# Seven block products for eight in gate and value: five sixths of a two-layer feed-forward kernel rewritten by Strassen's identity

## The chip, the cores and the metric

One core of one Trainium2 chip runs the program. The metric is device time in microseconds (us) of one execution; three runs of the kernel before stand beside one profiled execution.

## The reference, cut to what matters

```python
attn = softmax(mean_of_pairs(q) @ k.T / 8) @ v            # 2 x 8 heads, 1152 keys, 576 pooled queries
x = elu(x @ w_in) @ w_out                                 # 1152 tokens, 512 -> 2048 -> 512
xn = x / sqrt(mean(x * x) + 1e-6) * rms_g
g, val = xn @ w_gate, xn @ w_val                          # 512 -> 1536 each
out = (g * sigmoid(g) * val) @ w_out2                     # 1536 -> 512
```

The change is in the last two lines: `g` and `val`, and how their product is handed to the last matrix product.

## The kernel before, in words

Activations lie transposed: features on the 128 partitions, tokens along the free axis, in three chunks `c` of 384 tokens (`cs(c)`). Every fp32 product is made of three matmuls on rounded parts: an operand is split into a high part `h` (a cast) and a low part `l` (the rest), and `product` (L161) adds wh·xh, wh·xl and wl·xh over four blocks of 128 features: 12 matmuls of 128x384 for one 128-wide output block and one chunk. `xh`, `xl` hold the split input, `x2` the unsplit one.

The weights come as 64-bit words. `Stream` (L73) loads 68 blocks of 128x512 in the order of use and turns each into its two parts, in small steps that the loops call between products (`ws.step`): two ACT operations (L113 into `wt`, L115 into `we`), three DVE operations (L119, L121, L124, the last giving the block in fp32), a cast on ACT (L140, `wh`) and a subtraction on POOL (`lo_pool`, L63, `wl`). Eight blocks can be ready at once. Each engine runs its own queue in the order in which the program issues; a queue stands behind an instruction that waits.

After the first layer the last loop (L633) finishes `x2` chunk by chunk, and `Norm` scales it: `sums` (L572: three small matmuls, Sqrt on ACT, reciprocal on DVE), `spread` (L581: three transposes that lay the factor over the partitions) and `scale` (L587: four multiplications on DVE, four casts on ACT, four subtractions). For the last chunk this lies inside the next stage: `unit(0, 0)` and `unit(0, 1)` run first, with `sums` in the middle of the second, then `spread`, then the rest.

Gate and value: 12 output blocks `i`, three chunks. `unit(i, c)` (L661) is a gate and a value product, 24 matmuls; `swiglu` (L648) makes Silu on ACT, the product with the value on DVE, and the two parts `uh`, `ul` of the result (L657 on ACT, a subtraction on POOL or DVE). The last product reads `uh`, `ul` (L687). Eight PSUM banks go round (`bank`, L542).

Of the kernel before, what the change touches and what calls it, by code (L numbers as in the profile page):

```python
# [1 line left out]

# [6 lines left out]
F32 = mybir.dt.float32  # L9
# [29 lines left out]
def tile_kernel(ctx: ExitStack, tc: tile.TileContext, qd, kd, vd, w1d, w2d, wgd, wvd, wod, rgd, outd):  # L39
# [33 lines left out]
    class Stream:  # L73


        def __init__(self, srcs):
            self.srcs = srcs
            self.loaded = self.done = self.at = 0
            self.alloc = False
            self.raw, self.parts = {}, {}  # L80
            self.pools = [(wp, NE)]
            self.ops = self.work()
# [14 lines left out]
        def work(self):  # L97
            tail = None
            for i in range(len(self.srcs)):
                if tail and not wide:  # L100
                    yield from tail
                self.load(i + 2)
                w = self.raw.pop(i)
                if wide:

                    lo, hi = w[:, :, 0], w[:, :, 1]  # L110
                    e = wp.tile([128, 512], U32, tag="we", name="we", bufs=2)
                    t = wp.tile([128, 512], U32, tag="wt", name="wt", bufs=2)
# [11 lines left out]
                    V.scalar_tensor_tensor(out=t, in0=hi, scalar=0x80000000, in1=t,  # L124
                                           op0=ALU.bitwise_and, op1=ALU.bitwise_xor)
                    self.load(i + 3)
                    yield
                    w = f(t)
                tail = self.split(i, w)
                yield  # L130
            yield from tail

# [234 lines left out]
    def emit_x(p, xs, a=0, b=QS):  # L367
# [7 lines left out]
        else:  # L375
# [9 lines left out]
                + [w[i] for i in range(12) for w in (wgd, wvd)] + [wod[i] for i in range(12)])  # L385
# [156 lines left out]
    def bank():  # L542

        nonlocal nbank
        n, nbank = nbank % 8, nbank + 1
        if n == 5 and len(psb) == 1:
            with tc.using_default_side("right"):
                psb.append(ctx.enter_context(tc.tile_pool(name="psC", bufs=3, space=PSUM)))
        return psb[n >= 5].tile([128, 512], F32, tag="b", name="b", bufs=3 if n >= 5 else 5)[:, 0:CH]

    gh, gl = (gp.tile([128, 8, NT], F32R, name=f"g{n}", tag=f"g{n}") for n in "hl")

    def g_quad(hf, q, c):
        return lambda k: ((ge[0][:, k], ge[1][:, k]) if hf == c == q == 0 and k < NE else
                          (gh[:, 4 * q + k, cs(c)], gl[:, 4 * q + k, cs(c)]))

    class Norm:
# [14 lines left out]
        def sums(self):  # L572
            b = bank()
# [7 lines left out]
        def spread(self):  # L581

            b = self.b = bank()
# [16 lines left out]
    for hf in range(2):  # L600
        for i in range(8):
            w = ws.get(wi)
            for c in range(3):
# [4 lines left out]
                elu(ps, gh[:, i, cs(c)], gl[:, i, cs(c)], lo_dve if c == 1 and hf else lo_pool)  # L608
# [39 lines left out]
    def swiglu(i, c, pg, pv, k=4):  # L648
        s = hp.tile([128, CH], F32, tag="e", name="sl", bufs=4)
        T.activation(out=s, in_=pg, func=AF.Silu)  # L650
        flush()
        ws.step(wi + 2 * i if i > 1 else wi, k)
        V.tensor_tensor(out=s, in0=pv, in1=s, op=ALU.mult)

        def parts():
            h, l = uh[:, i, cs(c)], ul[:, i, cs(c)]
            T.copy(h, s)  # L657
            (lo_dve if c == 1 else lo_pool)(l, s, h)
        pending.append(parts)
# [8 lines left out]

    mctx.close()
    first = [unit(0, 0), unit(0, 1, norms[2].sums)]  # L670
# [10 lines left out]
    units = [(1, 0), (1, 1), (0, 2), (1, 2)] + [(i, c) for i in range(2, 12) for c in range(3)]  # L681
    for i, c in units:
        swiglu(*unit(i, c))
        ws.step(wi if i < 2 else wi + 2 * i, 3)
    wi += 24
    flush()
    for m in range(4):  # L687
        bs = [bank() for c in range(3)]
        for k in range(3):
            w = ws.get(wi)  # L690
            for c in range(3):
                product(bs[c], w, lambda b: (uh[:, 4 * k + b, cs(c)], ul[:, 4 * k + b, cs(c)]), k == 0, k == 2)
                ws.step(wi, 4)
                if k == 2:
                    o = hp.tile([128, CH], F32, tag="e", name="o", bufs=4)
                    T.copy(o, bs[c])
                    SP.dma_start(out=outd[128 * m:128 * m + 128, cs(c)], in_=o)
            wi += 1
# [56 lines left out]
```

## Time and profile before

| | us |
|---|---|
| three runs: median (lowest, highest) | 686.81 (686.01, 686.85) |
| the profiled execution, its own time | 686.79 |
| its span in the profile | 685.0 |
| busy PE, share of the span | 675.8, 99% |
| busy DVE, ACT, POOL | 469.0, 447.7, 376.1 |

A busy share says how much of the span an engine had something in work; for PE, whose matmuls overlap, the distance between two starts is the price of one. Gate and value start at 454.74 us of the span and the last product at 605.80 us.

### The profile page before, as it was taken

Reading aid. Unit: us, or ns where it says so; the run is one execution under the profiler, and the core shown is the slowest. Engines: PE = TensorE matmul, PEld = TensorE weight load, DVE = VectorE, ACT = ScalarE, POOL = GpSimd, SP = SyncE. Lnnn points to the kernel's source line nnn. Section 1 sums busy time; section 2 is a strip of 40 time slices with the busy share of each in tenths; the row PEclk is TensorE's granted clock in tenths of the full one; section 3 lists DMA queues with packets and bytes.
Section 4 is the critical chain, followed back from the end, with each engine's and each line's share of the span. In section 5 each row is a group of like instructions: output and inputs, shape, how many; then the busy total and the mean of one; then the engine's idle time right before and its main releaser. Section 6 shows DMA issues by size and latency. Waiting matters only on the chain.

```text
span 685.0 us, 11443 instructions
## 1 busy us (share of the span) xinstructions
PE 675.8 (99%) x4243; PEld 666.9 (97%) x4243; DVE 469.0 (68%) x752; ACT 447.7 (65%) x923; POOL 376.1 (55%) x335
## 2 busy tenths in 40 slices
PE   7999999999999999999999999999999999999997
PEld 6999999999999999999999999999999999999997
DVE  5989998998999875788557676377865655563000
ACT  5978889898988968885557875356655554453000
POOL 5798888898988415784324454464544443342000
PEclk9999999999999999999999999999999999999999
DMA  5522333233233001223421213112232222231000
GB/s 182 206 90 88 105 133 123 89 103 118 88 106 117 1 1 63 77 78 123 151 96 61 94 63 123 48 45 92 94 124 93 94 95 91 91 119 70 35 35 34
DMA packets 21608, 62.34 MB, mean 91 GB/s; under 512 B 2736, under 2 KB 4784, under 8 KB 21552
## 3 DMA queue, kind: packets, MB, share of 16 engines
q1 hardware_dynamic: 21552, 61.62, 26.8%
q8 instruction: 33, 0.54, 0.3%
q14 instruction: 23, 0.19, 0.1%
HBM read 59.25 MB, written 2.36 MB: 90 GB/s over the span
## 4 chain that ended last, share of the span: by engine, by line
PE 93%; POOL 3%; DMA 1%; ACT 1%; issue 1%; SPq 1%; POOLq 0%; ACTq 0%
PE b L166 20%; PE b L167 20%; PE b L168 20%; PE s L278 10%; PE o L322 10%; PE t L296 9%; DMA rawk<-in_k_dram 1%; POOL kd L63 1%; POOL vd L63 1%; PE t L357 1%; ACT p L287 1%; POOL qt L63 0%; POOL rawq L242 0%; PE fb L166 0%; PE fb L167 0%
## 5 line engine op out<-in xcount | busy, mean ns | idle before, releaser
L166 PE MATMUL b<-xh,wh 128*128 128x384 f32 x468 | 157.2, 336 | 0.0
L168 PE MATMUL b<-xh,wl 128*128 128x384 f32 x468 | 157.1, 336 | 0.0
L167 PE MATMUL b<-xl,wh 128*128 128x384 f32 x468 | 157.0, 335 | 0.0
L63 POOL TENSOR_TENSOR wl<-wt,wh 128x512 fp32r<-128x512 f32 x68 | 94.8, 1394 | 75.4 <-ACT wh L140 42.6
L282 DVE TENSOR_SCALAR_CACHE_REDUCE p<-s 128x1152 f32<-128x1152 f32 x72 | 97.4, 1354 | 18.1 <-PE s L278 17.7
L69 DVE TENSOR_TENSOR ptl<-t,pth 128x384 fp32r<-128x384 f32 x216 | 106.7, 549 | 4.3 <-ACT pth L304 3.4
L304 ACT CAST pth<-t 128x384 fp32r<-128x384 f32 x216 | 89.2, 488 | 24.4 <-PE t L296 23.6
L278 PE MATMUL s<-kd,qt 128*128 128x384 f32 x480 | 98.0, 341 | 3.2 <-DVE p L282 1.6
L287 ACT ACTIVATE p<-p,st 128x1152 f32<-128x1152 f32 x72 | 91.5, 1271 | 0.5 <-DVE p L282 0.2
L167 PEld LDWEIGHTS b<-xl,wh 128*128 128x128 f32 x468 | 87.9, 188 | 0.0
L166 PEld LDWEIGHTS b<-xh,wh 128*128 128x128 f32 x468 | 87.9, 188 | 0.0
L168 PEld LDWEIGHTS b<-xh,wl 128*128 128x128 f32 x468 | 87.9, 188 | 0.0
L296 PE MATMUL t<-ident,p 128*128 128x128 f32 x648 | 85.5, 275 | 1.3 <-ACT p L287 0.8
L278 PEld LDWEIGHTS s<-kd,qt 128*128 128x128 f32 x480 | 81.8, 188 | 4.9 <-POOL kd L63 2.0
L322 PE MATMUL o<-pth,vd 128*128 128x256 f32 (+1 forms) x288 | 84.4, 315 | 0.0
L296 PEld LDWEIGHTS t<-ident,p 128*128 128x128 f32 x648 | 73.9, 141 | 7.7 <-DVE ptl L69 4.7
L322 PE MATMUL o<-ptl,vd 128*128 128x256 f32 (+1 forms) x288 | 78.4, 294 | 0.0
L124 DVE SCALAR_TENSOR_TENSOR wt<-wr,wt 128x512 uint32<-128x512 uint32 x68 | 71.1, 1045 | 1.4
L121 DVE SCALAR_TENSOR_TENSOR wt<-wt,we 128x512 uint32<-128x512 uint32 x68 | 66.2, 973 | 6.5 <-ACT we L115 2.1
L113 ACT ACTIVATE wt<-wr 128x512 f32<-128x512 f32 x68 | 45.6, 671 | 36.9 <-POOL wl L63 20.3
L63 POOL TENSOR_TENSOR gl<-e,gh 128x384 fp32r<-128x384 f32 x37 | 42.1, 1138 | 41.2 <-ACT gh L187 39.8
L119 DVE TENSOR_SCALAR wt<-wt 128x512 f32<-128x512 f32 x68 | 48.9, 719 | 19.6 <-ACT wt L113 19.6
(111 smaller groups left out, 1303.2 us busy)
## 6 DMA issues: line engine op xcount, KB each, us to landing
wr<-in_w_dram SPq DMA_DIRECT2D x32, 512.0 KB, 3.2
rawk<-in_k_dram SPq DMA_DIRECT2D x32, 288.0 KB, 3.0
rawq<-in_q_dram SPq DMA_DIRECT2D x15, 576.0 KB, 4.1
wr<-in_wg_dram SPq DMA_DIRECT2D x12, 512.0 KB, 3.2
wr<-in_wv_dram SPq DMA_DIRECT2D x12, 512.0 KB, 3.2
wr<-in_wo_dram SPq DMA_DIRECT2D x12, 512.0 KB, 3.2
rawv<-in_v_dram SPq DMA_DIRECT2D x16, 288.0 KB, 2.8
out_dram<-o SPq DMA_DIRECT2D x12, 192.0 KB, 1.8
```

The source lines that it names most:

```text
L63: G.tensor_tensor(out=o, in0=i, in1=f(h), op=ALU.subtract)
L69: V.tensor_tensor(out=o, in0=i, in1=f(h), op=ALU.subtract)
L124: V.scalar_tensor_tensor(out=t, in0=hi, scalar=0x80000000, in1=t, op0=ALU.bitwise_and, op1=ALU.bitwise_xor)
L166: PE.matmul(out, lhsT=wh[:, k, :], rhs=ah, start=first and k == 0, stop=False)
L167: PE.matmul(out, lhsT=wh[:, k, :], rhs=al, start=False, stop=False)
L168: PE.matmul(out, lhsT=wl[:, k, :], rhs=ah, start=False, stop=last and k == 3)
L278: PE.matmul(s[:, m, 0:384], lhsT=a, rhs=b[:, 384 * m:384 * m + 384], start=n == 0, stop=n == len(parts) - 1)
L282: V.tensor_scalar(out=pt, in0=s[:, :, 0:384], scalar1=-0.0625, scalar2=None, op0=ALU.mult, op1=ALU.min, accum_out=st[p][:, 0, TILES[i][4], :])
L287: T.activation(out=pt, in_=pt, func=AF.Exp, scale=-1.0, bias=st[p][:, 0, TILES[i][4], :], accum_out=st[p][:, 1, TILES[i][4], :])
L296: PE.transpose(ps[:, k, :], src[:, 128 * b:128 * b + 128], ident)
L304: T.copy(oh, re(ps))
L322: PE.matmul(self.o[:, 0:self.N], lhsT=v[:, b, :], rhs=(pth, ptl)[u][:, g["buf"], b, g["c0"]:320], start=self.n == 0, stop=self.n == 17)
```

## The change

Of the 12 gate and value block pairs, pairs of output blocks (a `Branch`: two neighbouring blocks of gate, or of value) times chunks 0 and 1 form a 2x2 by 2x2 block product, over the halves of the 512 features. Branches 2 to 11 (five of the six pairs `i`) make it by the Winograd form of Strassen's identity: seven products of 6 matmuls in place of eight. Chunk 2, and the first pair for all chunks, stay as they were.

- Differences of the input, `t1` to `t4` (four DVE subtractions of 128x2x384, in place in `x2`, ahead of the last norm's `sums`), and their parts in `ts`.
- Four sums of the weights for each branch (`combine`: POOL, 128x256 each, into the single buffer `sf`), cast on ACT, 128x1024, and their low part on POOL, 128x1024, into one of three places.
- Additions on DVE behind the products (`u2`, `u3` and `out`).
- `u` stays unsplit fp32; from branch 10 on it is split in large pieces (`split_u`), into the room of `ts`, `xh`, `xl` and, for chunk 2, of `u0` and `u1`.
- The weights' intermediate `t` moves to a PSUM bank of its own (`wm`, one buffer), so seven banks go round; `wt` has three buffers; `spread` writes into the bank of `sums`; the order of the weights is gate, gate, value, value.

```diff
         def work(self):
...
                     e = wp.tile([128, 512], U32, tag="we", name="we", bufs=2)
-                    t = wp.tile([128, 512], U32, tag="wt", name="wt", bufs=2)
+                    w = wp.tile([128, 512], U32, tag="wt", name="wt", bufs=3)
+                    t = self.bank.tile([128, 512], U32, tag="wm", name="wm", bufs=1) if self.bank else w
...
+        def combine(self, n, a, b):
+            sf = mp.tile([128, 4, 256], F32, tag="sf", name="sf", bufs=1)
+            s1, s2, s3, s4 = (sf[:, k] for k in range(4))
+            a11, a12, a21, a22 = a[:, 0:256], a[:, 256:512], b[:, 0:256], b[:, 256:512]
+            G.tensor_tensor(out=s1, in0=a21, in1=a22, op=ALU.add)
+            yield
+            G.tensor_tensor(out=s2, in0=s1, in1=a11, op=ALU.subtract)
+            yield
+            G.tensor_tensor(out=s3, in0=a11, in1=a21, op=ALU.subtract)
+            yield
+            G.tensor_tensor(out=s4, in0=a12, in1=s2, op=ALU.subtract)
+            self.pair = n
+            yield
+            self.pair = None
+            h, l = self.place(n)
+            sf = sf.rearrange("p s (k c) -> p (s k) c", k=2)
+            T.copy(h, sf)
+            yield
+            lo_pool(l, sf, h)
+            self.sums[n] = (h, l)
+            yield
...
+    class Branch:
+        def group(self, out, a, b, first, last):
+            for k in range(2):
+                for x, y in ((0, 0), (0, 1), (1, 0)):
+                    PE.matmul(out, lhsT=a[x][:, k, :], rhs=b[y][:, k, :], start=first and (k, x, y) == (0, 0, 0),
+                              stop=last and (k, x, y) == (1, 1, 0), skip_group_check=True)
...
+            if n == 1:
+                self.a = bank()
+                self.group(self.a, a11, b11, True, False)
+                self.m1 = hp.tile([128, CH], F32, tag="e", name="m1", bufs=4)
+                T.copy(self.m1, self.a)
...
+            elif n == 6:
+                self.b = bank()
+                self.group(self.b, s(2), ts[1], True, False)
+                flush()
+                self.u2 = hp.tile([128, CH], F32, tag="e", name="u2", bufs=4)
+                V.tensor_tensor(out=self.u2, in0=self.b, in1=self.m1, op=ALU.add)
...
-    first = [unit(0, 0), unit(0, 1, norms[2].sums)]
+    first = [unit(0, 0)]
+    b11, b12, b21, b22 = (x2[:, 2 * j:2 * j + 2, cs(l)] for j in range(2) for l in range(2))
+    t1, t2, t3, t4 = b11, b22, b12, b21
+    for o, a, b in ((t1, b12, b11), (t3, b22, b12), (t2, b22, t1), (t4, b21, t2)):
+        V.tensor_tensor(out=o, in0=a, in1=b, op=ALU.subtract)
+    for n, t in ((2, t3), (1, t2), (3, t4)):
+        T.copy(ts[n][0], t)
+    lo_pool(ts[2][1], t3, ts[2][0])
+    first.append(unit(0, 1, norms[2].sums))
+    lo_dve(ts[1][1], t2, ts[1][0])
...
+    for n in range(2, 11):
+        b = Branch(n)
+        if old:
+            run([(b, 1), (old, 4), (b, 6), (old, 3)], n - 1, n + 2)
+        else:
+            run([(b, 1), (b, 6)], n, n + 2)
+        if n == 10:
+            split_u(0, 0, 3)
+        run([(b, k) for k in (5, 8, 7, 2, 9)], n, n + 3)
+        old = b
```

What moves on the queues stands in three places. The first is DVE around the last norm, where TensorE's `spread` waits for the reciprocal. In the kernel before:

```order
L619 TENSOR_TENSOR x_3521<-b,x_3521 128x384
L119 TENSOR_SCALAR wt<-wt 128x512
L579 RECIPROCAL rr<-rr 128x3
L653 TENSOR_TENSOR sl<-b,sl 128x384
L591 SCALAR_TENSOR_TENSOR x_3521<-x_3521,rg,b 128x384 x4
L69 TENSOR_TENSOR xl<-x_3521,xh 128x384 x2
L121 SCALAR_TENSOR_TENSOR wt<-wt,we 128x512
L124 SCALAR_TENSOR_TENSOR wt<-wr,wt 128x512
```

The same place of the same queue in the change:

```order
L662 TENSOR_TENSOR x_3524<-b,x_3524 128x384
L123 TENSOR_SCALAR wm<-wm 128x512
L789 TENSOR_TENSOR x_3524<-x_3524 128x2x384 x4
L622 RECIPROCAL rr<-rr 128x3
L70 TENSOR_TENSOR tsl<-x_3524,tsh 128x768
L776 TENSOR_TENSOR u_5629<-b,u_5629 128x384
L634 SCALAR_TENSOR_TENSOR x_3524<-x_3524,rg,b 128x384 x4
L70 TENSOR_TENSOR xl<-x_3524,xh 128x384 x2
L125 SCALAR_TENSOR_TENSOR wm<-wm,we 128x512
L128 SCALAR_TENSOR_TENSOR wt<-wr,wm 128x512
```

The four subtractions stand between the last addition of the first layer and the reciprocal, and one low part of 128x768 behind it. The second place is POOL, from the parts of the differences to the sums of branch 3 (the kernel before has one low part `wl` and one or two of `ul` in turn there):

```order
L64 TENSOR_TENSOR tsl<-x_3524,tsh 128x768
L64 TENSOR_TENSOR xl<-x_3524,xh 128x384 x2
L64 TENSOR_TENSOR tsl<-x_3524,tsh 128x768
L64 TENSOR_TENSOR wl<-wt,wh 128x512 x2
L146 TENSOR_TENSOR sf<-wt 128x256
L148 TENSOR_TENSOR sf<-sf,wt 128x256
L150 TENSOR_TENSOR sf<-wt 128x256
L152 TENSOR_TENSOR sf<-wt,sf 128x256
L64 TENSOR_TENSOR sl<-sf,sh 128x1024
L64 TENSOR_TENSOR wl<-wt,wh 128x512 x2
```

Two low parts of weights, four sums and a low part of the sums now follow each other, once for each branch. The third is ACT, from the cast of the first sums (L158) to that of the next:

```order
L158 CAST sh<-sf 128x1024
L774 ACTIVATE u_5747<-b 128x384
L117 ACTIVATE wm<-wr 128x512
L119 ACTIVATE we<-wr 128x512
L171 CAST wh<-wt 128x512
L774 ACTIVATE u_5747<-b 128x384
L117 ACTIVATE wm<-wr 128x512
L119 ACTIVATE we<-wr 128x512
L728 COPY m_5839<-b 128x384
L171 CAST wh<-wt 128x512
L158 CAST tsh<-sf 128x1024
```

Each L158 waits for POOL's four sums, and what ACT does for the next weights, L117 first, stands behind it.

## Rows read from the trace of the kernel before

**Rows 1.** The page's part 1: engines, busy us, share, count.

```profile
span 685.0 us, 11443 instructions
...
PE 675.8 (99%) x4243; PEld 666.9 (97%) x4243; DVE 469.0 (68%) x752; ACT 447.7 (65%) x923; POOL 376.1 (55%) x335
```

**Rows 2.** The page's part 4, the chain that ended last, by engine.

```profile
PE 93%; POOL 3%; DMA 1%; ACT 1%; issue 1%; SPq 1%; POOLq 0%; ACTq 0%
```

**Rows 3.** Timeline of PE: start, us, what; gate and value, its ends.

```profile
454.74 0.34 PE L166 MATMUL b<-xh,wh 128*128 128x384 f32 x1
...
463.73 0.49 PE L585 MATMUL b<-ident,rr 128*128 128x128 f32 x3
...
505.76 0.35 PE L166 MATMUL b<-xh,wh 128*128 128x384 f32 x1
...
605.80 0.34 PE L166 MATMUL b<-uh,wh 128*128 128x384 f32 x1
```

**Rows 4.** Groups of PE by line and form, 455 to 686 us.

```profile
L166 PE MATMUL b<-xh,wh 128*128 128x384 f32 x288 | 96.8, 336 | 0.0
```

**Rows 5.** Busy time by engine (count), PEclk, DMA, 505.9 to 605.9 us.

```profile
505.90:605.90 100.00, 100.00 (x578) 100.00 (x577) 58.77 (x87) 51.86 (x103) 40.94 (x34) 1.00 0.28 95
```

**Rows 6.** Timeline of DVE around the last norm.

```profile
457.97 0.41 DVE L119 TENSOR_SCALAR wt<-wt 128x512 f32<-128x512 f32 x1
462.04 0.18 DVE L579 RECIPROCAL rr<-rr 128x3 f32<-128x3 f32 x1 [3.65 <-ACT rr L578]
463.93 0.56 DVE L653 TENSOR_TENSOR sl<-b,sl 128x384 f32<-128x384 f32 x1 [1.72 <-ACT sl L650]
...
466.50 1.86 DVE L69 TENSOR_TENSOR xl<-x,xh 128x384 fp32r<-128x384 f32 x2
...
469.00 0.69 DVE L124 SCALAR_TENSOR_TENSOR wt<-wr,wt 128x512 uint32<-128x512 uint32 x1
```

**Rows 7.** Timeline of ACT around the last norm.

```profile
461.74 0.26 ACT L578 ACTIVATE rr<-b,eps 128x3 f32<-128x3 f32 x1 [2.62 <-PE b L575]
462.02 1.28 ACT L671 ACT_TABLE_LOAD   x1
...
463.43 0.47 ACT L650 ACTIVATE sl<-b 128x384 f32<-128x384 f32 x1
```

**Rows 8.** Timeline of POOL around the last norm.

```profile
458.75 1.01 POOL L570 TENSOR_TENSOR sq<-sq,sqm 128x384 f32<-128x384 f32 x1 [1.59 <-ACT sqm L568]
459.72 1.29 POOL L63 TENSOR_TENSOR wl<-wt,wh 128x512 fp32r<-128x512 f32 x1
```

**Rows 9.** Groups of DVE by form, 440 to 485 us: count, busy us, mean ns.

```profile
L69 DVE TENSOR_TENSOR xl<-x,xh 128x384 fp32r<-128x384 f32 x6 | 5.9, 996 | 0.2
...
L69 DVE TENSOR_TENSOR ul<-sl,uh 128x384 fp32r<-128x384 f32 x2 | 1.1, 552 | 1.7 <-ACT uh L657 1.7
```

**Rows 10.** Groups of ACT by form, 480 to 600 us.

```profile
L113 ACT ACTIVATE wt<-wr 128x512 f32<-128x512 f32 x23 | 15.5, 675 | 14.6 <-POOL wl L63 9.0 <-DMA wr<-in_wv_dram 3.3 <-DMA wr<-in_wg_dram 2.3
L650 ACT ACTIVATE sl<-b 128x384 f32<-128x384 f32 x30 | 14.7, 489 | 41.6 <-PE b L168 41.6
...
L115 ACT ACTIVATE we<-wr 128x512 uint32<-128x512 uint32 x22 | 14.6, 662 | 0.0
L140 ACT CAST wh<-wt 128x512 fp32r<-128x512 f32 x22 | 13.5, 613 | 0.2
```

**Rows 11.** Groups of POOL by form, whole span.

```profile
L63 POOL TENSOR_TENSOR wl<-wt,wh 128x512 fp32r<-128x512 f32 x68 | 94.8, 1394 | 75.4 <-ACT wh L140 42.6 <-issue 21.2 <-DVE wt L121 3.8
...
L242 POOL TENSOR_TENSOR rawq<-rawq 128x256 f32<-128x256 f32 x1 | 1.3, 1299 | 5.8 <-DMA rawq<-in_q_dram 5.8
L63 POOL TENSOR_TENSOR qt<-rawq,qt 128x256 fp32r<-128x256 f32 x1 | 0.7, 729 | 0.1
```

**Rows 12.** Groups of DVE by form, 480 to 600 us.

```profile
L121 DVE SCALAR_TENSOR_TENSOR wt<-wt,we 128x512 uint32<-128x512 uint32 x23 | 26.2, 1137 | 1.8
...
L653 DVE TENSOR_TENSOR sl<-b,sl 128x384 f32<-128x384 f32 x30 | 16.7, 555 | 30.5 <-PE b L168 30.5
```

More of the change, by code (lines that the diff above doesn't have):

```diff
@@ L1 @@
 from contextlib import ExitStack
+from itertools import chain
 import concourse.bass as bass
@@ L79, in __init__ @@
             self.alloc = False
-            self.raw, self.parts = {}, {}
+            self.bank = None
+            self.pairs_from, self.pairs, self.limit, self.pair = len(srcs), 0, 0, None
+            self.raw, self.parts, self.sums = {}, {}, {}
             self.pools = [(wp, NE)]
@@ L157, in get, with get_sums @@
             return self.parts[i]
+        def get_sums(self, n):
+            while n not in self.sums:
+                next(self.ops)
+            return self.sums[n]
     cs = lambda c: slice(c * CH, (c + 1) * CH)
@@ L384, in tile_kernel @@
                              (w_in[8:16] if hf else w_in[NE:8]) + [w_out[4 * (2 * hf + q) + m] for m in range(4) for q in range(2)]]
-                + [w[i] for i in range(12) for w in (wgd, wvd)] + [wod[i] for i in range(12)])
+                + [w[2 * i + n] for i in range(6) for w in (wgd, wvd) for n in range(2)] + [wod[i] for i in range(12)])
+    ws.pairs_from, ws.pairs = 32, 12
+    ws.place = lambda n: sums_at[n % 3]
     LT = 2
@@ L572, in sums @@
         def sums(self):
-            b = bank()
+            b = self.b = bank()
             for n in range(3):
@@ L581, in spread @@
         def spread(self):
-            b = self.b = bank()
+            b = self.b
             for n in range(3):
@@ L680, in tile_kernel @@
     ws.step(wi, 1)
[L681 to L684, printed above, removed]
+    units = [unit(1, 0), unit(1, 1)]
+    swiglu(*units[0])
+    ws.step(wi, 3)
+    T.copy(ts[0][0], t1)
+    lo_dve(ts[0][1], t1, ts[0][0])
+    swiglu(*units[1])
+    gctx.close()
+    with tc.using_default_side("right"):
+        u2p = ctx.enter_context(tc.tile_pool(name="u2", bufs=1))
@@ new lines, in tile_kernel, with run, parts @@
+    u.append(u2p.tile([128, 12, CH], F32, name="u2", tag="u2"))
+    sums_at.append([u2p.tile([128, 8, 128], F32R, name=f"s{a}", tag=f"s{a}") for a in "hl"])
+    ws.limit = 5
+    ws.step(wi, 3)
+    for i in range(2):
+        swiglu(*unit(i, 2))
+        ws.step(wi, 3)
+    def run(order, i, limit, k=2):
+        ws.limit = limit
+        for br, m in order:
+            br.m(m)
+            ws.step(wi + 2 * i, 3 * k if m > 7 else k)
+    def parts(c, j, n=1):
+        if c == 1:
+            a = slice(j % 4, j % 4 + n)
+            return [t[:, a, cs(j // 4)] for t in (xh, xl)]
+        a = (j + 6) % 12 if c == 0 else j
+        return [t[:, a:a + n] for t in ((th, tl) if c == 0 else us)]
@@ L685, in tile_kernel @@
+    run([(b, 1), (old, 4), (b, 6), (old, 3)], 10, 12, 1)
+    split_u(0, 3, 3, lo_pool)
+    run([(b, 5), (b, 7)], 11, 12, 0)
+    split_u(0, 6, 3)
+    run([(b, 2), (b, 8), (b, 4)], 11, 12, 0)
+    split_u(0, 9, 3)
+    run([(b, 3)], 11, 12, 0)
+    split_u(1, 0, 4, lo_pool)
+    split_u(1, 4, 4)
+    run([(b, 9)], 11, 12, 0)
+    flush()
+    split_u(1, 8, 4)
     wi += 24
-    flush()
     for m in range(4):
         bs = [bank() for c in range(3)]
[L689 to L698, printed above, removed]
+        for c, k in ([(c, k) for c in range(3) for k in range(3)] if m == 0 else [(c, k) for k in range(3) for c in range(3)]):
+            if (m, c, k) == (0, 0, 0):
+                uctx.close()
+                fp = ctx.enter_context(tc.tile_pool(name="u2s", bufs=1))
+                us = [fp.tile([128, 12, CH], F32R, name=f"us{a}", tag=f"us{a}") for a in "hl"]
+            w = ws.get(wi + k)
+            product(bs[c], w, lambda b: [t[:, 0] for t in parts(c, 4 * k + b)], k == 0, k == 2)
+            if m == c == 0:
+                split_u(2, 4 * k, 4, lo_pool if k == 1 else lo_dve)
+            ws.step(wi + (k if m else 0), 4)
+            if k == 2:
+                o = hp.tile([128, CH], F32, tag="e", name="o", bufs=4)
+                T.copy(o, bs[c])
+                SP.dma_start(out=outd[128 * m:128 * m + 128, cs(c)], in_=o)
+        wi += 3
```

115 lines of the change are left out of this document (91 added, 24 removed).

## The prediction

> **What bounds the kernel now.** I read the page from the top. TensorE is busy for 99% of the span, every other engine for at most 68% [rows 1], and the chain that ended last runs through PE for 93% of its length [rows 2]. Then I asked where the change sits. Gate and value last from 454.74 to 605.80 us, and PE waits for nothing there [rows 3]: its groups show no idle time [rows 4], and in the hundred microseconds from 505.9 on it is busy for all of them, at the full granted clock of 1.00, while DVE has 58.8 us of work, ACT 51.9 and POOL 40.9 [rows 5]. So this stage costs its number of matmuls times the price of one, and the other engines have room as long as nothing of theirs comes late. The price of one isn't the 336 ns of a row [rows 4]: matmuls overlap, and what counts is the distance between starts. From the first matmul of block 4 to the first of the last product there are 8 blocks of 72, in 605.80 - 505.76 = 100.04 us [rows 3]: 0.1737 us each.
>
> **What it removes.** A branch had 4 products of 12 on chunks 0 and 1; it gets 7 of 6, that is 42 for 48. Ten branches save 60 matmuls, and the program's TensorE list is 60 shorter: 60 x 0.1737 = **10.4 us**. Since PE waits for nothing, all of it is gain if PE still waits for nothing. A branch then lasts 66 x 0.1737 = 11.5 us (chunk 2 keeps its 24).
>
> **What it adds ahead of the spread.** In the kernel before DVE ends its L119 at 458.38 and stands idle until the reciprocal at 462.04; the transposes start at 463.73, when PE reaches them [rows 3, 6]. Now four subtractions of 128x768 go into that gap, and behind them on ACT three casts ahead of the Sqrt. No row has 128x768 with two SBUF inputs. The nearest is the low part of 128x384: 0.55 us where POOL is quiet and 1.00 where it works [rows 9], so about 1.0 or 2.0 us for twice the length. In this stretch POOL has a sum of squares (1.0), a weight's low part (1.3) [rows 8] and the low part of a difference (some 2.3), so I take two at 1.0 and two at 2.0: they end at 464.4. The last cast (0.9, from 0.61 for 128x512 [rows 10]), Sqrt 0.26 [rows 7] and reciprocal 0.18 [rows 6], with the steps between, put the spread at 465.7: a wait of **2.0 us**. All quiet gives 0, all slow gives 4.0.
>
> Here a page bears on the price. By the Trainium skill, SBUF — State Buffer, Who interferes with whom, a DVE instruction with two SBUF inputs and a GpSimd instruction that reads SBUF exclude each other, and the second to issue blocks until the first ends. By that rule subtractions and POOL's three instructions would take turns, 4.0 + 4.6 us from 458.4, and the wait would be 3.3 in place of 2.0, the total 1.3 later. The row of 1.00 us agrees in kind [rows 9].
>
> **What it adds ahead of the first sums.** Write S for the end of the spread (464.22 before [rows 3]). The chain behind S decides when branch 2 gets its sums, and nothing of it can start earlier. Because the Sqrt now comes just before S, the table load and the Silu behind it (1.9 us together [rows 7]) end at S+1.3, where the multiplication had begun at S-0.3 [rows 6]; the block of weights whose third operation ended at 469.69 [rows 6], S+5.5, ends at S+7.1. From there, in the order of the queues: ACT's L117, L119 and a Silu to S+8.8; the multiplication that DVE holds for that Silu (0.5) and two operations on the second block (0.7 each, the quiet price [rows 6]) to S+10.7; L117, L119 and a cast to S+12.5 [rows 10]; POOL's low part of that block, 1.4 [rows 11], to S+13.9; four sums of 128x256. One row of that size is 0.73, another 1.30 [rows 11]; I take 0.75, since most DVE operations of this stretch have one SBUF input or none, and 0.4 for the one low part of 128x768 on DVE: S+17.3. The cast of 128x1024 is 1.1, from 0.61 for half [rows 10], and the low part of 128x1024 2.6, from 1.39 for half [rows 11]: S+21.0. PE reaches the matmul that reads this part after 4 x 24 + 6 + 2 = 104 matmuls, at S+18.1. It waits **3.0 us** (1.0 with an early Silu and quiet sums, 5.5 with sums at 1.30 and the low part at 2.9).
>
> **The ring behind it.** From one cast of sums to the next, ACT, DVE and POOL hand the work round, because ACT stands at that cast until POOL's sums are done, and the next L117 stands behind it: L117 0.6, Silu 0.45, L119 0.6, two DVE operations 1.4, then L117, L119 and cast 1.8, low part 1.4, sums 3.0, cast 1.1, and a copy or Silu 0.5, in all 10.9 us against PE's 11.5. The second sums are ready at S + 18.4 + 10.9 + 2.6 = S+31.9; PE, let go at S+21.0, wants them 60 matmuls later, at S+31.4: **0.5 us** (0 to 2). From then on the ring gains 0.6 us per branch on PE, and I count nothing more.
>
> **What I cost at nothing.** The additions (5 of 0.55 us per branch [rows 12]) and Silu, m1 copies and casts on ACT: per branch DVE has some 9 us and ACT some 7 of 11.5; DVE's largest branch, of value, some 10. If that cover goes, the ring shows it. Seven banks for eight: a bank comes round after six products of 2.1 us, 12.5 us, and is held by about 1.5 us of ACT and DVE work. The split of `u` at the end: from the last product on chunk 0 DVE has 9.5 us of it at quiet prices, up to 16, and PE has 15.6 us of matmuls before it needs the last of it: 0, at most 1.5. One PSUM buffer for the weights' intermediate makes ACT wait for DVE's third operation, in a chain of 3 us per block where a block is wanted every 5.7 at most.
>
> **The sum.** The profiled execution took 686.79 us, next to the median of 686.81. 686.79 - 10.4 + 2.0 + 3.0 + 0.5 = **681.9 us**.
>
> **The rivals.** (a) *No waits*: the subtractions run at the quiet price and the first sums are in time to within a microsecond. DVE's 3.65 us of idle time [rows 6] is nearly long enough for four times 1.0; against it, the first sums end a serial chain in which only POOL's prices can shrink. 677.5 us, chance 0.22. (b) *The ring is the bound*: if POOL's sums cost 1.1 us each, between the two rows of that size, the ring takes 12.4 us, PE waits 0.9 in each of eight more branches, and the first wait grows by 1.4: 681.9 + 7.2 + 1.4 = 690.5, slower than before. It decides from a ring of 12.0 on, which with the first wait grown is even with before; with sums at 1.30 it would be 698. Against it: DVE's operations on the weights, where rows show 1.14 us with two SBUF inputs against a quiet 0.69 [rows 6, 12], lose one SBUF input to PSUM. Chance 0.10. (c) *More waits at the seams*: all four subtractions slow, or the split of `u` late, 2 to 4 us more: 685.5, chance 0.08. That the identity doesn't shorten PE's list is excluded by the list itself.
>
> By the same section of the Trainium skill, an instruction with at most one SBUF input doesn't contend, which speaks for the quiet price in the ring; were it wrong and the 1.14 us [rows 12] stayed, the ring would take 11.4 and the 0.6 us of gain per branch be gone, at no other cost.
>
> **How the numbers follow.** My forecast, waits of 3 to 8 us in all, has a chance of 0.60, and 681.9 us. The range reaches down into (a), to 677.0, and up into (c), to 686.5; most of (b) lies outside. A measurement of this kernel can tell 0.2%, 1.4 us, from no change. Faster by more than that: the forecast, (a) and a little of (c), 0.84; within it 0.07; slower 0.09.
>
> **What would show it.** Right: PE's matmuls at 0.174 us apart in branches 4 to 11 with no idle time; one wait of about 2 us at the transposes, ended by DVE's reciprocal; one of about 3 us in the first product that reads sums, ended by POOL's low part. Wrong: waits for `sl` or `tsl` in most branches (the ring); POOL's sums far from 0.75 us; DVE's operations on `wm` no shorter than those on `wt` were; waits for `ush` or `usl` in the last product.

## The result and the profile after

| | before | changed |
|---|---|---|
| runs: median (lowest to highest), us | 686.47 (686.01 to 686.85) | 696.85 (695.34 to 696.9) |
| ratio, 95% interval | | 1.0146 [1.0129, 1.0164] |
| span of the profiled execution, us | 685.0 | 695.0 |

The change makes the kernel 1.5% slower, where 681.9 us, some 0.7% faster, was forecast; the range ended at 686.5.

Names in the rows of after: L204 to L206 is `product`, L702 a group of the block product, L628 the spread's transposes, L622 the reciprocal, L774 a Silu of `swiglu`, L158 the cast of the sums, L728 the copy of m1, L751 and L756 `u2` and `u3`, L709 and L715 the additions of `out`, L717 the product with Silu, L840 the casts of `split_u`, L64 and L70 low parts on POOL and DVE.

The page's parts 1 and 4 of after (span, busy time of each engine, chain of waits by engine), against [rows 1, 2]:

```profile
span 695.0 us, 11426 instructions
...
PE 672.4 (97%) x4183; PEld 659.1 (95%) x4183; DVE 476.7 (69%) x803; ACT 460.4 (66%) x921; POOL 410.8 (59%) x366
...
PE 71%; DVE 9%; POOL 8%; ACT 6%; issue 3%; DMA 1%; SPq 0%; DVEq 0%; POOLq 0%; ACTq 0%
```

The list is 60 matmuls shorter, as said. But PE is no longer alone on the chain: 71% for 93%, the rest handed to DVE, POOL and ACT, none of which is busy for more than 69%. Where PE stands is in the view of its waits, of after from 455 us on (what waits, what released it, us in all, times, longest):

```profile
PE b L702 <- DVE u L751: 3.7, 3, 1.6
PE b L628 <- DVE rr L622: 2.7, 1, 2.7
PE b L702 <- POOL sl L64: 2.6, 2, 1.8
PE b L205 <- POOL usl L64: 2.2, 1, 2.2
PE b L702 <- DVE u L756: 1.5, 1, 1.5
PE b L205 <- DVE usl L70: 0.9, 1, 0.9
PE b L204 <- ACT u L774: 0.2, 1, 0.2
```

Before, there was no wait in this stage. The list makes 13.8 us of them; a restart costs another 0.1 to 0.2, since the second matmul too starts late. So I counted on PE's timeline by how much the distance between two starts exceeds 0.1737 us a matmul, wherever by over 0.02, from 453.6 us on. This count, in us, is used for every kernel below:

| | up to the first sums (492 us) | branches 3 to 9 (to 588) | branches 10, 11 (to 612) | last product | lower clock | sum |
|---|---|---|---|---|---|---|
| before | 0.2 | 0 | 0 | 0 | 0 | 0.2 |
| after | 5.9 | 4.6 | 3.6 | 3.8 | 1.5 | 19.4 |
| forecast | 5.0 | 0.5 | 0 | 0 | 0 | 5.5 |

686.8 - 10.4 + 19.4 = 695.8 us, within 1.1 of the median. So the saving came whole, to about 1 us, and waits took it back nearly twice.

The column of the lower clock is the stretch behind the last two waits. PE's timeline of after shows the waits, then starts 0.32 us apart (the 1.2 GHz level) from 629.87 to 633.07, then 0.17 again; the row of windows has the granted clock at 0.89 for these 15 us:

```profile
624.43 0.44 PE L205 MATMUL b<-usl,wh 128*128 128x384 f32 x1 [0.95 <-DVE usl L70]
...
628.99 0.44 PE L205 MATMUL b<-usl,wh 128*128 128x384 f32 x1 [2.17 <-POOL usl L64]
...
630.19 0.52 PE L204 MATMUL b<-ush,wh 128*128 128x384 f32 x1
630.51 0.52 PE L205 MATMUL b<-usl,wh 128*128 128x384 f32 x1
...
633.27 0.34 PE L205 MATMUL b<-usl,wh 128*128 128x384 f32 x1
```

```profile
620.00:635.00 15.00, 11.88 (x57) 11.21 (x56) 10.22 (x12) 8.94 (x12) 8.30 (x4) 0.89 0.22 77
```

### The profile page after: what moved, and what is told of

Its sections match the earlier page's. It is cut to its first block, busy times and chain, and to the rows that moved or that the text cites. A ratio compares the mean times of both kernels' runs of the same rounds, so it can differ in the third digit from the quotient of the medians.

```text
span 695.0 us, 11426 instructions
## 1 busy us (share of the span) xinstructions
PE 672.4 (97%) x4183; PEld 659.1 (95%) x4183; DVE 476.7 (69%) x803; ACT 460.4 (66%) x921; POOL 410.8 (59%) x366
## 4 chain that ended last, share of the span: by engine, by line
PE 71%; DVE 9%; POOL 8%; ACT 6%; issue 3%; DMA 1%; SPq 0%; DVEq 0%; POOLq 0%; ACTq 0%
PE b L205 13%; PE b L206 13%; PE b L204 13%; PE s L316 11%; PE o L360 10%; PE t L334 9%; DVE u L717 2%; PE b L702 2%; POOL wl L64 2%; DVE wm L125 1%; DVE wt L128 1%; ACT we L119 1%; DVE x L789 1%; ACT wm L117 1%; POOL sf L152 1%
## 5 line engine op out<-in xcount | busy, mean ns | idle before, releaser
L64 POOL TENSOR_TENSOR wl<-wt,wh 128x512 fp32r<-128x512 f32 x68 | 91.8, 1351 | 89.6 <-ACT wh L171 76.6
L204 PE MATMUL b<-xh,wh 128*128 128x384 f32 x356 | 120.2, 338 | 0.2 <-ACT u L774 0.2
L206 PE MATMUL b<-xh,wl 128*128 128x384 f32 x356 | 119.8, 336 | 0.0
L205 PE MATMUL b<-xl,wh 128*128 128x384 f32 x356 | 119.8, 336 | 0.0
L70 DVE TENSOR_TENSOR ptl<-t,pth 128x384 fp32r<-128x384 f32 x216 | 106.7, 549 | 3.4 <-ACT pth L342 2.6
L123 DVE TENSOR_SCALAR wm<-wm 128x512 f32<-128x512 f32 x62 | 43.0, 694 | 40.3 <-ACT wm L117 40.3
L204 PEld LDWEIGHTS b<-xh,wh 128*128 128x128 f32 x356 | 67.0, 188 | 0.7 <-ACT u L774 0.5
L205 PEld LDWEIGHTS b<-xl,wh 128*128 128x128 f32 x356 | 67.0, 188 | 0.1
L206 PEld LDWEIGHTS b<-xh,wl 128*128 128x128 f32 x356 | 67.0, 188 | 0.0
L117 ACT ACTIVATE wm<-wr 128x512 f32<-128x512 f32 x62 | 39.2, 633 | 38.2 <-DVE wt L128 28.4
L64 POOL TENSOR_TENSOR gl<-e,gh 128x384 fp32r<-128x384 f32 x37 | 38.8, 1053 | 42.3 <-ACT gh L225 42.3
L204 PE MATMUL b<-gh,wh 128*128 128x384 f32 x180 | 61.0, 339 | 0.0
L206 PE MATMUL b<-gh,wl 128*128 128x384 f32 x180 | 60.6, 337 | 0.0
```

Of the source, the lines that this page charges most:

```text
L64: G.tensor_tensor(out=o, in0=i, in1=f(h), op=ALU.subtract)
L70: V.tensor_tensor(out=o, in0=i, in1=f(h), op=ALU.subtract)
L204: PE.matmul(out, lhsT=wh[:, k, :], rhs=ah, start=first and k == 0, stop=False)
L205: PE.matmul(out, lhsT=wh[:, k, :], rhs=al, start=False, stop=False)
L206: PE.matmul(out, lhsT=wl[:, k, :], rhs=ah, start=False, stop=last and k == 3)
```

## The experiments

Two theories were put against each other. **A**: each wait comes from one place in one queue, and goes when that place is mended. **B**: POOL, ACT and DVE together set the pace, and a wait that is removed comes back at the next place.

### The split at the end

Why is `usl` late? The last product's wait follows from these rows of after, DVE and then POOL (start, us, what, idle time before it and what ended it):

```profile
613.14 0.55 DVE L715 TENSOR_TENSOR v<-b,u 128x384 f32<-128x384 f32 x1
613.73 3.49 DVE L717 TENSOR_TENSOR u<-v,u 128x384 f32<-128x384 f32 x1
617.14 1.74 DVE L70 TENSOR_TENSOR xl<-u,xh 128x1536 fp32r<-128x1536 f32 x1
```

```profile
613.29 3.51 POOL L64 TENSOR_TENSOR xl<-u,xh 128x1536 fp32r<-128x1536 f32 x1 [6.38 <-DVE tsl L70]
623.17 2.34 POOL L64 TENSOR_TENSOR wl<-wt,wh 128x512 fp32r<-128x512 f32 x1 [6.38 <-ACT wh L171]
625.48 3.46 POOL L64 TENSOR_TENSOR usl<-u,ush 128x1536 fp32r<-128x1536 f32 x1
```

L717 with both operands in SBUF takes 3.49 us and ends 0.4 after POOL's 3.51 us on `xl`, which began before it; the L715 ahead of it, with one operand in PSUM, takes 0.55. This is the lock that the prediction took from the Trainium skill, SBUF — State Buffer, Who interferes with whom, and the trace agrees with it in full length, where I had allowed for a factor of two at most. ACT's cast of `xh` waits for that product, DVE's `xl` for the cast, `ush` for `xl` because it lies in the room of `u1`, and POOL, busy with a weight's low part until 625.5, needs 3.46 for its `usl`.

First only the two pieces on POOL went to DVE (e3):

```diff
-    split_u(1, 0, 4, lo_pool)
+    split_u(1, 0, 4)
...
-                split_u(2, 4 * k, 4, lo_pool if k == 1 else lo_dve)
+                split_u(2, 4 * k, 4)
```

> Two of the large low parts of u (128x1536, chunk 1 first quarter and chunk 2 second quarter) move from POOL to DVE. Theory A (POOL's 3.5 us instruction holds a DVE multiplication with two SBUF inputs, which took 3.49 us, and the casts of chunk 2 stand behind it): that multiplication falls to about 0.56, the two waits in the last product (0.95 and 2.17 us) shrink to under 1 us together, and the stretch at the lower clock behind them (about 1.8 us) goes too: 3 to 5 us less, about 693. Rival (the split is late because ACT and DVE have too much of it): DVE has 3.5 us more, the waits stay within 1 us of what they were.

Measured 696.35 us, 1.0145 [1.013, 1.016]: no gain that can be told, and 3.8 us of waits there as in after. L717 is back at 0.56, but the third cast of `ush` now stands behind ACT's L117, which waits 4.02 us for the weights' one PSUM buffer:

```profile
626.30 0.64 ACT L117 ACTIVATE wm<-wr 128x512 f32<-128x512 f32 x1 [4.02 <-DVE wt L128]
626.87 1.46 ACT L840 CAST ush<-u 128x1536 fp32r<-128x1536 f32 x1
```

So e7 also takes the weights' steps from between the three pieces:

```diff
-            if m == c == 0:
-                split_u(2, 4 * k, 4)
+            if m == c == k == 0:
+                for j in (0, 4, 8):
+                    split_u(2, j, 4)
```

> All low parts of u's split in the last four tiles on VectorE instead of two on POOL, and the three parts of chunk 2 straight one behind the other, with no step of the weights between them. Theory A: VectorE's product of two operands in SBUF is back at 0.56 us from 3.49, ScalarE's third cast no longer stands behind an activation that waits 4 us, and of the 3.1 us of waits in the last product some 0.3 are left; the stretch at the lower clock behind them (1.8 us) goes with them: 692.2 us, or 693.8 if the clock falls all the same. Theory B: the weights of the last stage come late in place of the split: 696 us.

Measured 691.51 us, 1.0073 [1.0058, 1.0088], 5.3 us less: the 3.5 us of waits there (0.3 are left) and the 1.5 of lower clock behind them; up to the first sums this execution has 1.1 less of waits and 1.0 of lower clock in their place. Theory A holds here for the two edits together. How much is the lock's and how much the order's isn't shown: e3 took the lock away and gained nothing, and the order by itself, with POOL's pieces left, was not run.

### The copy of m1

The waits for `u2` in branches 8 and 9 come about as ACT's and DVE's timelines of after show for branch 8.

```profile
557.52 0.60 ACT L171 CAST wh<-wt 128x512 fp32r<-128x512 f32 x1
562.64 1.05 ACT L158 CAST tsh<-sf 128x1024 fp32r<-128x1024 f32 x1 [4.53 <-POOL sf L152]
563.60 0.47 ACT L728 COPY m<-b 128x384 f32<-128x384 f32 x1
```

```profile
561.31 0.69 DVE L128 SCALAR_TENSOR_TENSOR wt<-wr,wm 128x512 uint32<-128x512 uint32 x1
564.10 0.56 DVE L751 TENSOR_TENSOR u<-b,m 128x384 f32<-128x384 f32 x1 [2.10 <-ACT m L728]
```

The copy's matmuls ended at 556.78, but it stands behind the cast, which stands 4.53 us for POOL's last sum of the next branch. Over 480 to 600 us, ACT stands 39.9 us ahead of these ten casts, and DVE 13.0 us ahead of L751 for the copy (groups by form):

```profile
L751 DVE TENSOR_TENSOR u<-b,m 128x384 f32<-128x384 f32 x9 | 5.0, 557 | 13.0 <-ACT m L728 13.0
```

```profile
L158 ACT CAST tsh<-sf 128x1024 fp32r<-128x1024 f32 x6 | 6.3, 1052 | 23.2 <-POOL sf L152 23.2
...
L728 ACT COPY m<-b 128x384 f32<-128x384 f32 x10 | 4.7, 469 | 0.0
...
L158 ACT CAST sh<-sf 128x1024 fp32r<-128x1024 f32 x4 | 4.2, 1050 | 16.7 <-POOL sf L152 16.7
```

So the copy went to DVE (e2):

```diff
-                T.copy(self.m1, self.a)
+                V.tensor_copy(self.m1, self.a)
```

> The copy of the first product (m1) runs on DVE instead of ACT, where it stood behind the cast of the sums. Theory A: the waits of TensorE for u2 and u3 (L751, L756: 3.7 + 1.5 us, with restarts about 6) go, although DVE gets 0.55 us more work in each of ten branches; the time falls by 4 to 6 us, to about 692. Theory B (these additions are late because DVE or the ring is short of time): the waits stay or grow, and the time changes by less than 1.5 us or rises.

Measured 693.12 us, 1.0103 [1.0087, 1.0119], 3.7 us less. The same groups of this kernel: DVE no longer waits for m1, and the copy costs it 0.55 us.

```profile
L728 DVE COPY m<-b 128x384 f32<-128x384 f32 x10 | 5.5, 550 | 0.6 <-PE b L702 0.6
...
L751 DVE TENSOR_TENSOR u<-b,m 128x384 f32<-128x384 f32 x10 | 5.5, 548 | 0.1
```

Branches 3 to 9 lose 1.2 us for 4.6 and wait once, 0.3; the casts of sums come every 10.94 us (484.14 to 582.6, nine steps), so the ring has room, as forecast. In all this execution counts some 7 us less of waits (2.4 up to the first sums, 3.4 in branches 3 to 9, 1.5 in the last product) and 5.1 us at the lower clock for 1.5. Of the 2.4, most is the clock's doing: POOL's low part of the first sums ends at 487.67 for 488.01 in after, but PE, 2.3 us later by the lower clock, no longer waits for it.

### Where the subtractions stand

The first column's 5.9 us were attacked in four orders. First the subtractions, their casts and one low part went behind the last norm's sums (e1):

```diff
+    first.append(unit(0, 1, norms[2].sums))
     for o, a, b in ((t1, b12, b11), (t3, b22, b12), (t2, b22, t1), (t4, b21, t2)):
...
-    first.append(unit(0, 1, norms[2].sums))
     lo_dve(ts[1][1], t2, ts[1][0])
```

> The four subtractions, their casts and the low part of t3 are issued behind the last norm's sums instead of ahead of them; nothing else. Theory A (separate waits, each from one place of a queue): the wait at the transposes (2.7 us, ended by DVE's reciprocal) goes, the first sums come some 0.5 us later against S, so the time falls by 1.5 to 2.7 us, to about 694.6. Theory B (the ring of POOL, ACT and DVE bounds the stage, and a wait removed comes back at the next place): the wait at the transposes goes, the waits in branches 2 to 11 grow by as much, and the time falls by less than 1 us.

Measured 698.03 us, 1.0169 [1.0154, 1.0184]. The wait at the transposes is gone and PE waits 2.1 and 1.4 us for banks that a Silu has to free, the first of them because that Silu now stands behind the casts of the differences. So in e6 they went behind the first Silu and its product:

```diff
     norms[2].spread()
     swiglu(*first[0], 0)
+    for o, a, b in ((t1, b12, b11), (t3, b22, b12), (t2, b22, t1), (t4, b21, t2)):
+        V.tensor_tensor(out=o, in0=a, in1=b, op=ALU.subtract)
...
     norms[2].scale()
```

> The four subtractions, the casts of the differences and two low parts stand behind the first Silu and its product instead of ahead of the last norm's sums. Theory A (each wait stands by itself): the 2.7 us at the transposes go with 0.1 for the restart, no wait for a bank as in the run with the subtractions behind the sums only (2.1 and 1.4 us there): 694.0 us. Theory B (the ring of POOL, ACT and DVE sets the pace, a removed wait comes back): the wait at the first sums grows from 2.0 to about 4.5 us, for POOL's sums start no earlier: 696.5 us or more.

Measured 698.18 us, 1.0171 [1.0155, 1.0187]: now the second Silu is late, in one wait of 5.1 us. In e8 this order was put together with the two edits that had gained, and in e9 with three more (m8 ahead of m6 in branch 2, `split_u(0, 0, 3)` moved into branch 11, m8 ahead of m7 there):

> The copy of m1 on VectorE (693.1 us by itself), the subtractions behind the first Silu and the end of e7 together. Theory A: 693.1 less 2.8 (transposes) less 2.4 (lower clock behind them in that run) less 2.3 (last product) less 1.8 (lower clock behind it) makes 683.8 us, below the kernel before. Theory B: no better than 690 us, with waits for sums in several branches.

> As e8, and besides: m8 ahead of m6 in the first branch, the first part of u's split (0.0 to 0.2) moved from branch ten into branch eleven, and m8 ahead of m7 in the last branch. Theory A: the waits for u2 and u3 in branches ten and eleven (1.1 and 1.9 us, and 1.5 of lower clock behind them) go too: 679 us; with every wait gone and the clock full it would be 676.5. Theory B: above 686 us.

Measured 689.84 us, 1.0045 [1.0029, 1.0062], and 690.01 us, 1.0052 [1.0037, 1.0067]. Theory A's 683.8 and 679 were missed, and the waits for sums that theory B had in several branches did not come either. The 5.1 us at one place came along, and behind them the lower clock, 0.77 in this row of e8's windows:

```profile
470.00:485.00 15.00, 9.88 (x42) 9.56 (x41) 11.83 (x18) 8.21 (x15) 8.38 (x7) 0.77 0.21 70
```

The third order lets the second Silu and five steps of the weights go ahead of the casts, with t4 behind the norm's scaling; alone (e10), with the edits of e2 and e7 (e11), and with an edit of branches 10 and 11 besides (e12):

```diff
+    for o, a, b in ((t1, b12, b11), (t3, b22, b12), (t2, b22, t1)):
+        V.tensor_tensor(out=o, in0=a, in1=b, op=ALU.subtract)
+    swiglu(*first[1], 0)
+    ws.step(wi, 5)
+    for n, t in ((2, t3), (1, t2)):
+        T.copy(ts[n][0], t)
...
     norms[2].scale()
```

> Only the order behind the last norm's sums differs from the changed kernel: three subtractions, and then the second Silu with its product and five steps of the weights, stand ahead of the casts of the differences, the fourth subtraction behind the last norm. Theory A: the 2.7 us at the transposes, and the 5.1 us for the Silu's bank that the earlier two orders had in their place, are both gone: 694.0 us. Theory B: POOL's sums of branch two are ready no earlier than in the changed kernel, so the first sums wait 4 to 5 us instead of 2.0: 696 us.

> The order of the run before, with m1's copy on VectorE and the mended split at the end (which with the older order took 689.8 us and had 5.1 us at one bank and 3.4 us of lower clock behind it). Theory A: 689.8 less 5.4 less 3.4 makes 681.0 us. Theory B: 3 to 4 us of it come back at the first sums: 684.5 us. Either way below the kernel before.

> As the run before, and the first part of u's split moved from branch ten into branch eleven, and the steps of the weights in branch eleven moved from its first four groups behind m5 and m7. Theory A: the waits for u3 and u2 in branches ten and eleven (1.2 and 1.9 us, 0.3 for restarts) go: 677.6 us where the run before gives 681.0. Theory B: a wait of 1 to 2 us shows at another place of branch eleven: within 1 us of the run before.

Measured 697.52 us (1.0165 [1.0147, 1.0183]), 693.69 us (1.0101 [1.008, 1.0123]) and 691.6 us (1.0072 [1.0057, 1.0087]). Theory B describes this stretch: e10's waits are 1.6 us for the last norm's `xl`, 1.9 for the sums' cast and 1.8 for their low part, 7.0 us in all, and 2.7 at the lower clock besides. They came along into e11, so that it missed both theories' figures by 9 us and more. The seam's edits in e12 took 1.7 of the 3.5 us in branches 10 and 11 (less than A's 3.4). By the medians they are worth 2.1 us, but e11's four runs lie 2.9 us apart, and e15, which has them over e14, gained 1.55:

```diff
-        if n == 10:
-            split_u(0, 0, 3)
...
-    run([(b, 1), (old, 4), (b, 6), (old, 3)], 10, 12, 1)
+    run([(b, 1), (old, 4), (b, 6), (old, 3)], 10, 12, 0)
+    split_u(0, 0, 3)
     split_u(0, 3, 3, lo_pool)
-    run([(b, 5), (b, 7)], 11, 12, 0)
+    run([(b, 5), (b, 7)], 11, 12, 2)
```

The fourth order (e13) puts subtractions, casts and low parts behind the norm's scaling, ahead of `swiglu(*units[0])`. Alone it gives PE an undisturbed path to branch 2:

> The subtractions, the casts of the differences and their low parts stand behind the last norm's scaling and behind both products of the first block pair's units, and the low parts of the differences are all VectorE's. Theory A: the wait at the transposes goes and nothing that PE needs before branch two stands behind them: 694.0 us. Theory B, now for the stretch from the last norm to the first sums alone: the three engines have more work there than PE leaves time for, as the three orders before showed, and 4 to 5 us of waits stand ahead of the first sums and the first differences: 696.5 us.

Measured 699.65 us, 1.0182 [1.0165, 1.0198]. PE arrives with no wait, and waits 6.05 us for the sums' cast and 1.43 for the low part: the sums are ready at 490.28 us of the trace, in after at 488.07. That is worse than either theory had it.

Then the stretch was to get more of PE's work as cover, all with the edits of e2 and e7: with this order (e14), with the seam (e15), and with the changed kernel's order again (e16):

```diff
-            run([(b, 1), (b, 6)], n, n + 2)
+            run([(b, 1), (b, 8), (b, 2), (b, 9), (b, 6)], n, n + 2)
...
```

> The order of the run before with m1's copy on VectorE, the mended end, and in the first branch m8, m2 and m9 (30 matmuls, 5.2 us) ahead of m6, so that sums and differences are wanted 5.2 us later. Theory A: 691.5 (the end by itself) less 3.7 (m1's copy by itself) less 2.8 (transposes) less 2.3 (first sums) makes 682.7 us. Theory B: the cover is used up at the next branch, whose sums and third difference come late: 687 us.

> The run before, and in branches ten and eleven the split's first part and the steps of the weights moved as in e12, which took 2.1 us off there. Theory A: 680.6 us. Theory B: 686 us.

> The run before, with subtractions, casts and low parts back in the place that the changed kernel has them (ahead of the sums of the last norm). Theory A: 2.8 us for the wait at the transposes, and up to 2.4 if the clock falls behind it, come on top of the run before: 683.4 to 685.8 us. Theory B: the same time as the run before, since then the ring and not the wait sets it.

Measured 694.05 us (1.0106 [1.0091, 1.0121]), 692.5 us (1.0079 [1.0064, 1.0094]) and 691.7 us (1.0067 [1.005, 1.0084]). e14 and e15 are above both theories' figures. The cover was badly chosen: m2 adds into the bank that m1's copy reads, so PE waits for the copy, 6.96 us in e14 and 2.16 in e16. That e16 is no slower than e15 again fits B.

What is too much there? e19 leaves the subtractions out of the changed kernel:

> The changed kernel without its four subtractions: x's own blocks stand in for the differences, and casts, low parts and all matmuls stay. If VectorE's 7.1 us of subtractions are what is too much between the last norm and the first sums, the reciprocal comes at 461 us of the trace instead of 466.5 and everything behind it 4 to 5 us earlier, and both waits go: 696.9 less 2.8 less 2.3 makes 691.8 us. If POOL's sums set the first sums by themselves, only the wait at the transposes goes and the one at the first sums grows to 4.5 us: 696.5 us.

Measured 690.95 us, 1.0072 [1.0057, 1.0087], 5.9 us less. Nothing waits up to the first sums; they are ready at 483.53 us for 488.07, and PE waits 1.34 us for them. Casts and low parts are all still there. So it is the subtractions on DVE that push the reciprocal, the scaling, the weights and by these POOL's sums back. Of the 5.9 us the count gives the stretch 4.1 and the lower clock 1.5: the end's waits are the same in this execution, but no lower clock follows them.

### Branch 2, and what gained put together

In branch 2 alone, m8 ahead of m6 (e4):

```diff
-            run([(b, 1), (b, 6)], n, n + 2)
+            run([(b, 1), (b, 8), (b, 6)], n, n + 2)
...
```

> In branch 2 the first product of chunk 2 (12 matmuls, 2.1 us) runs ahead of the first product that reads sums. Theory A: the wait for the first sums (1.83 us and 0.3 before it) falls to 0 to 0.4 and the time by about 2 us, to 694.9. Theory B: PE then arrives 2 us earlier at the later sums and additions, and waits for them instead: less than 1 us gained.

Measured 695.45 us, 1.0129 [1.0112, 1.0146], 1.4 us less, though the runs of the two kernels overlap; the first sums' wait went, and 1.44 us came back at the second sums. Last, the edits that had gained, with the subtractions where the changed kernel has them (e17); and the same with t4 on POOL (e18):

> The subtractions stay where the changed kernel has them. Together: m1's copy on VectorE (3.7 us by itself), the mended end (5.4 by itself), m8 ahead of m6 in the first branch (1.4 by itself) and the seam of branches ten and eleven (2.1 between two runs that have all else alike). Theory A (the waits are separate, their prices add): 696.9 less 12.6 makes 684.3 us, below the kernel before. Theory B (they come back in the next branches): 687.5 us or more.

> The run before, and the fourth subtraction on POOL instead of VectorE, its cast behind the first Silu. VectorE reaches the reciprocal some 1.8 us earlier and ScalarE's root no longer stands behind the third cast, so the wait at the transposes falls from 2.7 to about 0.5 us. Theory A: 2.2 us under the run before. Theory B for the stretch up to the first sums: the sums and the third difference's low part come no earlier, and the run before's time stays within 0.7 us.

Measured 686.92 us, 1.0007 [0.9998, 1.0016], and 687.26 us, 1.0012 [1.0003, 1.0021]. Of 12.6 us that the single edits promised, 9.9 came, between the two theories' figures. e17 counts 4.0, 3.3, 1.8 and 0.4 us of waits, no lower clock, 9.6 in all: about the 10.4 that 60 matmuls are worth, and so it equals the kernel before. Its waits:

```profile
PE b L628 <- DVE rr L622: 2.7, 1, 2.7
PE b L702 <- POOL tsl L64: 1.7, 1, 1.7
PE b L702 <- DVE u L751: 1.3, 1, 1.3
PE b L204 <- DVE v L715: 0.4, 1, 0.4
PE b L204 <- ACT u L774: 0.2, 1, 0.2
PE b L702 <- POOL sl L64: 0.2, 1, 0.2
```

In e18 the wait at the transposes fell from 2.67 to 0.15, as expected, 1.1 came back at a Silu's bank and 1.4 at `u3` of the seam: theory B's figure. No version beat the kernel before.

## Why the prediction was wrong

- *What it removes*: right. 60 matmuls fewer, and 686.8 - 10.4 plus the counted sum comes within 1.5 us of every kernel's median, but for e11 (2.1) and e13 (2.4), whose profiled executions were 2.0 and 1.9 us faster than their medians.
- *Ahead of the spread*, 2.0 us (0 to 4.0): measured 2.67, 2.9 with the restart. The four subtractions took 7.10 us in place of 6.0 (after; DVE, then POOL, then the casts on ACT that wait for the last three):

```profile
458.38 7.10 DVE L789 TENSOR_TENSOR x<-x 128x768 f32<-128x768 f32 x4
```

```profile
458.62 1.57 POOL L613 TENSOR_TENSOR sq<-sq,sqm 128x384 f32<-128x384 f32 x1 [1.64 <-ACT sqm L611]
460.16 2.00 POOL L64 TENSOR_TENSOR wl<-wt,wh 128x512 fp32r<-128x512 f32 x1
462.11 2.56 POOL L64 TENSOR_TENSOR tsl<-x,tsh 128x768 fp32r<-128x768 f32 x1
```

```profile
461.05 0.83 ACT L791 CAST tsh<-x 128x768 fp32r<-128x768 f32 x1 [2.05 <-DVE x L789]
463.01 0.84 ACT L791 CAST tsh<-x 128x768 fp32r<-128x768 f32 x1 [1.13 <-DVE x L789]
465.52 0.83 ACT L791 CAST tsh<-x 128x768 fp32r<-128x768 f32 x1 [1.68 <-DVE x L789]
```

The last three subtractions end at 461.01, 462.97 and 465.49, just ahead of these casts and each 0.8 us behind the end of one of POOL's instructions, and took 1.58, 1.85 and 2.48 us; the first, which began ahead of POOL's, took 0.94. Three of them took 3.07 us in e11, where POOL was idle. So the quiet price of 1.0 was right, and the other case has no fixed price: DVE and POOL took turns. The 1.00 us that the contended 2.0 was doubled from is a mean of six [rows 9], two of 0.56 and four of 1.09 to 1.36. The prediction's sum for taking turns has a slip: 4.0 + 4.6 us from 458.4 ends at 467.0, which makes a wait of 4.6 and not 3.3.

- *Ahead of the first sums*, 3.0 us: measured 1.83, and 0.28 at `sh` before it. The serial chain was right; sums of 0.74 us, a cast of 1.05 and a low part of 2.4 were as priced (POOL's groups by form, 480 to 600 us: count, busy us, mean ns).

```profile
L152 POOL TENSOR_TENSOR sf<-wt,sf 128x256 f32<-128x256 f32 x10 | 7.8, 775 | 0.0
L150 POOL TENSOR_TENSOR sf<-wt 128x256 f32<-128x256 f32 x10 | 7.4, 738 | 0.0
```

- *DVE's operations on `wm`*: 0.69 to 0.70 us each (the two lines, DVE of after, 480 to 600 us, by form), where L121 had 1137 ns [rows 12]. So moving one input to PSUM did end that contention; L123 pays for it with 0.69 us, where its predecessor had 0.41 in SBUF [rows 6]. By the Trainium skill, VectorE: DVE Perf Modes, Why PSUM operands drop a tier, a PSUM operand holds an fp32 operation at the lowest rate; the two rows agree.

```profile
L125 DVE SCALAR_TENSOR_TENSOR wm<-wm,we 128x512 uint32<-128x512 uint32 x22 | 15.4, 698 | 2.3 <-ACT we L119 1.1
L123 DVE TENSOR_SCALAR wm<-wm 128x512 f32<-128x512 f32 x22 | 15.2, 692 | 10.0 <-ACT wm L117 10.0
```

- *The ring*: its period was forecast as 10.9 us and is 10.94 in e2, and the wait for the second sums was 0.3 for 0.5. Rival (b) did not happen. **The step that failed** is "From then on the ring gains 0.6 us per branch on PE, and I count nothing more", with "What I cost at nothing" behind it: I added up each engine's work (DVE 9 us, ACT 7 of 11.5) and took what fits for hidden. m1's copy fits ACT's time and yet came some 5 us late, because the ring itself keeps ACT standing at the cast, and the copy is behind it in the queue. Branches 3 to 9 lost 4.6 us, of which moving that one instruction took away 3.4.
- *The split of `u`*: "0, at most 1.5" was the second failed step: 3.8 us in the last product, 1.5 at the lower clock behind it, and with the work of `split_u` in DVE's queue between the weights a part of the 3.6 in branches 10 and 11 (e12 took 1.7 off there). DVE's work lay within what I said (9.5 us, up to 16). What I had not followed is the chain through ACT, DVE and POOL and the room of `u1`, on which each piece waits for the last. In it one DVE product was held for nearly the whole 3.5 us of a POOL instruction, but ending that alone gained nothing (e3); with the order mended too, 3.5 of the 3.8 went (e7). By the count this step cost more than the first, 5.3 us and a part of the 3.6, for 4.1. The lower clock had no term in the forecast at all.
- *Rival (c)*, more waits at the seams, had two of the places, the subtractions and the split of `u`, but not the copies of m1; it was priced at 2 to 4 us and given 0.08. The sum of what was missed, 19.4 - 5.5 = 13.9 us, makes 681.9 + 13.9 = 695.8.

What stays open: whether an order exists in which the subtractions are hidden. Each order that keeps the subtractions left 2.3 (e18) to 8.9 us (e13) of waits up to the first sums, and what e18 gained there came back later. That the wait in branch 3 of e17 (1.7 us) comes from the same chain was not tried.

## What to carry to other kernels

An engine that is busy half of the time can still be late (ACT, 62.7 of the 120 us from 480 on): for each instruction that the bottleneck waits for, ask what stands ahead of it in its queue and how long that one stands, not how full the engine is. A short copy must not be queued behind an instruction that waits for a long chain of other engines. Where a kernel runs its bottleneck at 99% with no wait, a change that saves matmuls by adding work elsewhere has to pay for each new place where it can wait; here that took the whole gain even after mending (9.6 us of 10.4 in e17).

## What was not expected of the hardware

A stretch at the lower clock can follow a short wait of PE and cost half as much again or more: in after, starts were 0.32 us apart for 3.2 us (1.5 us lost), beginning 0.9 us after the restart from a wait of 2.17; in e2, 2.3 us were lost behind one of 2.7. And it need not come: e19 has the same two waits at the end, of 0.96 and 2.17 us, and its windows show the clock at 1.00, while e2 has 0.86 behind the wait at the transposes where after has 1.00 (windows of e19, then e2, then after):

```profile
615.00:630.00 15.00, 11.87 (x66) 11.19 (x65) 10.31 (x11) 8.64 (x12) 7.80 (x4) 1.00 0.20 62
```

```profile
455.00:480.00 25.00, 22.34 (x116) 22.02 (x115) 19.52 (x26) 14.62 (x27) 14.10 (x10) 0.86 0.15 57
```

```profile
455.00:470.00 15.00, 12.33 (x75) 12.02 (x74) 12.74 (x16) 8.27 (x15) 8.00 (x5) 1.00 0.08 30
470.00:485.00 15.00, 14.84 (x86) 14.52 (x84) 10.97 (x17) 7.41 (x15) 10.56 (x9) 1.00 0.20 70
```

In the traces of the changed kernel and its variants these stretches make 0 to 5.1 us, so a few us of difference between two of them can be the clock's; the count of waits and of clock apart tells which. What decides whether the clock falls behind a wait isn't shown.
